# Pool's layer norm adds a negated mean instead of subtracting the mean, on one Trainium2 core

## The chip, the cores and the metric

The kernel runs on one core of one Trainium2 chip. The metric is the device time of one execution in microseconds (us). The engines are called PE (matmul), PEld (its weight loads), DVE (vector), ACT (scalar), Pool (GpSimd) and SP (which here only issues DMAs). Several chips were used. Kernels are compared with runs of the kernel before on the same chip, in the same rounds; where two runs of different chips are set side by side, the text says so. Faster, same, slower is taken at 2%, so a clear difference below that counts as "same".

## The reference, cut to what matters

The input x is 2048 tokens by 448 features. It is layer-normalised once (xn) and then goes through a linear-attention branch and an MLP-mixer branch that has a second layer norm.

```python
def _layernorm(x, axis=-1, eps=1e-5):
    m = jnp.mean(x, axis=axis, keepdims=True)
    v = jnp.var(x, axis=axis, keepdims=True)
    return (x - m) / jnp.sqrt(v + eps)
...
x = A_x
xn = _layernorm(x, axis=-1)
return x + _A_ref(xn, ...) + _B_ref(xn, ...)     # _B_ref: x1 = xn + hs; gelu(_layernorm(x1) @ w3) @ w4
```

## The kernel before

The tokens are 16 tiles of 128. One layer norm of a tile is: statistics on DVE (`bn_stats`, `bn_aggr`), variance plus epsilon on DVE, the power -1/2 on Pool, and the apply (x - mean) * rstd, which is one instruction on DVE or on Pool.

```python
def ln_stats(stt, mvt, src, i):
    R.ew(dve, "bn_stats", stt[:, i, 0:6], src[:, i, 0:D])
    R.ew(dve, "bn_aggr", mvt[:, i, 0:2], stt[:, i, 0:6])

def ln_scale(mvt, rst, a, n):
    R.ew(dve, "tensor_scalar", mvt[:, a:a + n, 2], mvt[:, a:a + n, 1], LN_EPS, 1.0, op0=ALU.add, op1=ALU.mult)
    R.ew(pool, "tensor_tensor", rst[:, a:a + n, 0], mvt[:, a:a + n, 2], mhalf[:, 0:n], op=ALU.pow)

def ln_apply(eng, dst, src, mvt, rst, i):
    R.ew(eng, "tensor_scalar", dst, src, mvt[:, i, 0:1], rst[:, i, 0:1], op0=ALU.subtract, op1=ALU.mult)
```

In the first norm DVE applies tiles 0 to 3. From tile 4 on, tiles go in pairs, and Pool applies the even tile of each pair (6 applies) and DVE the odd one. In the second norm Pool does all 16 applies; their results are called g_tok. SP transposes g_tok by DMA into gT, which feeds the w3 matmuls.

```python
for i in range(4, NT, 2):
    ln1_stats(i, 2)
    ln1_apply(i, 1, [pool])
    if i > 4:
        ln1_apply(i - 1, 1, [dve])
ln1_apply(NT - 1, 1, [dve])
...
def g_apply(i):
    ln_apply(pool, halves(g_tok[:, i % 4, :]), lap(xn[:, i, :]), mv2, rs2, i)
def g_T(i):
    R.dma_t(gT[:, (i // 4) % 2, :, j:j + 128], g_tok[:, i % 4, :])
```

Most tiles of xn are transposed by PE, but tiles 12 to 15 go by DMA, at the end of the first norm. The normalising of phik and of the attention output (o_tok, a part of the tile xnT) are also Pool's work.

The softmax here doesn't subtract the row's maximum and nothing guards it: scores larger than these inputs give would overflow.

Of the kernel before, what the change touches and what calls it, by code (L numbers as in the profile page):

```python
# [5 lines left out]
ACT = mybir.ActivationFunctionType  # L6
ALU = mybir.AluOpType
# [4 lines left out]
LN_EPS = 1e-5  # L12
# [5 lines left out]
class Recorder:  # L18
# [183 lines left out]
    def dma_t(self, out, in_, eng="SP"):  # L202
        self.op(eng, lambda e: e.dma_start_transpose(out, in_), [out], [in_], dma=True)

    def dma(self, out, in_, eng="SP"):
        self.op(eng, lambda e: e.dma_start(out, in_), [out], [in_], dma=True)


def bass_parallel_sum__linear_kernel_hedgehog__mixer_s_mlp__prompt_kernel(
# [6 lines left out]
    NT, NG, KC, NC, NM, FC, HP = 16, 4, 4, 4, 4, 14, 32  # L216
# [6 lines left out]
    with es:  # L223
        R = Recorder(nc, es)
# [13 lines left out]
        def new(name, cols, dt=BF16):  # L238
            return view(region(name, cols * DTB[dt]), cols, dt)
# [9 lines left out]
        xtok = new("xtok", NT * D).rearrange("p (t d) -> p t d", t=NT)  # L249
        xn = new("xn", NT * 512).rearrange("p (t d) -> p t d", t=NT)  # L250
# [13 lines left out]
        wv = new("wv", KC * D).rearrange("p (c d) -> p c d", c=KC)  # L264
# [17 lines left out]
        mv = new("mv", NT * 8, F32).rearrange("p (t c) -> p t c", t=NT)  # L282
        rs = new("rs", NT * 8, F32).rearrange("p (t c) -> p t c", t=NT)
        st2 = new("st2", NT * 8, F32).rearrange("p (t c) -> p t c", t=NT)
        mv2 = new("mv2", NT * 8, F32).rearrange("p (t c) -> p t c", t=NT)
        rs2 = new("rs2", NT * 8, F32).rearrange("p (t c) -> p t c", t=NT)
        ksum = new("ksum", 4 * 32, F32).rearrange("p (b c) -> p b c", b=4)
        rks = new("rks", 4 * 32, F32).rearrange("p (b c) -> p b c", b=4)
        mhalf = new("mhalf", 8, F32)
# [33 lines left out]
        dve, pool = "DVE", "POOL"  # L323
# [6 lines left out]
            R.dma(dst[:, 0:3, :], src[0:384, :].rearrange("(c p) d -> p c d", p=128))  # L330
            R.dma(dst[0:64, 3, :], src[384:448, :])

        def load_lap(dst, src, eng="SP"):
            R.dma(dst[:, 0:2, :], src[0:256, :].rearrange("(c p) d -> p c d", p=128), eng)
            R.dma(dst[:, 2:4, :], src[192:448, :].rearrange("(c p) d -> p c d", p=128), eng)

        load_x(0, 1)
# [13 lines left out]
        def load_rest():  # L351
# [7 lines left out]
        kq = kvq[0:CR, :, :].rearrange("p b (h e) -> p b h e", e=HP)  # L359

        R.op("ACT", lambda e: e.preload_act_table_set("gelu_apprx_tanh_and_others"), [], [])
        load_lap(wv, A_wqkv[:, 896:1344], "ACT")
        R.ew(pool, "memset", ident[:, :], 0.0)
        R.op(pool, lambda e: e.affine_select(ident[:, :], ident[:, :], pattern=[[-1, 128]],
                                             compare_op=ALU.not_equal, fill=1.0, base=0, channel_multiplier=1),
             [ident], [ident])
        R.ew(pool, "memset", mhalf[:, :], -0.5)
        R.ew(pool, "memset", hT[:, :, 0:2], 0.0)
        R.ew(pool, "memset", hT[:, :, S + 2:S + 4], 0.0)
        R.ew(pool, "memset", vp[:, 0:8 * H, DH:HP], 0.0)  # L370
        R.ew(pool, "memset", vp[:, 0:8 * H, DH:DH + 1], 1.0)
        def masks():
            R.ew(pool, "memset", rsel[0:DH, :], 0.0)
            R.op(pool, lambda e: e.affine_select(rv, rv, pattern=[[0, 4], [-1, DH]], compare_op=ALU.not_equal,
                                                 fill=1.0, base=0, channel_multiplier=1), [rsel[0:DH, :]], [rsel[0:DH, :]])
            R.ew(pool, "memset", maskb[0:CR, :], 1.0)
            R.op(pool, lambda e: e.affine_select(mb, mb, pattern=[[-DH, 4], [0, DH]], compare_op=ALU.is_ge,
                                                 fill=0.0, base=0, channel_multiplier=1), [maskb[0:CR, :]], [maskb[0:CR, :]])
            R.op(pool, lambda e: e.affine_select(mb, mb, pattern=[[DH, 4], [0, DH]], compare_op=ALU.is_ge,
                                                 fill=0.0, base=DH - 1, channel_multiplier=-1),  # L380
                 [maskb[0:CR, :]], [maskb[0:CR, :]])
# [12 lines left out]
        def lap(a):  # L394
            return bass.AP(a.tensor, a.offset, [list(a.ap[0]), [192, 2], [1, 256]])

        def halves(a):
            return a.rearrange("p (b e) -> p b e", b=2)

        def ln_stats(stt, mvt, src, i):  # L400
            R.ew(dve, "bn_stats", stt[:, i, 0:6], src[:, i, 0:D])
            R.ew(dve, "bn_aggr", mvt[:, i, 0:2], stt[:, i, 0:6])

        def ln_scale(mvt, rst, a, n):
            R.ew(dve, "tensor_scalar", mvt[:, a:a + n, 2], mvt[:, a:a + n, 1], LN_EPS, 1.0, op0=ALU.add, op1=ALU.mult)
            R.ew(pool, "tensor_tensor", rst[:, a:a + n, 0], mvt[:, a:a + n, 2], mhalf[:, 0:n], op=ALU.pow)

        def ln_apply(eng, dst, src, mvt, rst, i):
            R.ew(eng, "tensor_scalar", dst, src, mvt[:, i, 0:1], rst[:, i, 0:1], op0=ALU.subtract, op1=ALU.mult)

        def ln1_stats(a, n):
            for i in range(a, a + n):
                ln_stats(st, mv, xtok, i)
            ln_scale(mv, rs, a, n)

        def ln1_apply(a, n, engs):
            for i in range(a, a + n):
                ln_apply(engs[i % len(engs)], halves(xn[:, i, :]), lap(xtok[:, i, :]), mv, rs, i)


        def phi_blocks():
# [13 lines left out]
        def xn_T(i, b):  # L435
            b = banks[b]
            for kc in range(KC):
                R.tr(tview(b)[:, 128 * kc:128 * kc + 128], xn[:, i, 128 * kc:128 * kc + 128], ident[:, :])
            R.act(xnT[:, :, 128 * i:128 * i + 128], tview(b).rearrange("p (c d) -> p c d", c=KC), ACT.Copy)
# [39 lines left out]
        def kq_quad(i, bs):  # L479
            g, c = divmod(i, 4)  # L480

            def outs(k):
                return banks[bs[k]][:, 0:D] if k < 2 else banks[bs[k]][0:CR, :]

            def lhs(k, kc, lo, hi):
                if k < 2:
                    return xnT[lo:hi, kc, 128 * (i + k):128 * (i + k) + 128]
                return wpq[lo:hi, kc, CR * (c + k - 2):CR * (c + k - 1)]

            def rhs(k, kc, lo, hi):  # L490
                return wpk[lo:hi, kc, :] if k < 2 else xnT[lo:hi, kc, 512 * g:512 * g + 512]

            quad(outs, lhs, rhs)
            for s in range(2):
                R.act(phik[:, i:i + 2, s, :], two(bs[0])[:, :, 0:D], ACT.Exp, scale=1.0 - 2.0 * s)
            e = (eq_lo if g < 2 else eq_hi)[0:CR, c:c + 2, :, 512 * (g % 2):512 * (g % 2) + 512]
            for s in range(2):
                R.act(e[:, :, s, :], two(bs[2])[0:CR, :, :], ACT.Exp, scale=1.0 - 2.0 * s)
# [41 lines left out]
        def g_apply(i):  # L540
            ln_apply(pool, halves(g_tok[:, i % 4, :]), lap(xn[:, i, :]), mv2, rs2, i)
# [71 lines left out]
            R.dma(out2d[128 * i:128 * i + 128, :], outb[:, i % 4, :])  # L613


        for i in range(4):
            ln1_stats(i, 1)
            if i > 0:
                ln1_apply(i - 1, 1, [dve])
        ln1_apply(3, 1, [dve])  # L620
        masks()
        for i in range(4, NT, 2):
            ln1_stats(i, 2)
            ln1_apply(i, 1, [pool])
            if i > 4:
                ln1_apply(i - 1, 1, [dve])
        ln1_apply(NT - 1, 1, [dve])
        xn_T(0, 0)
        xn_T(1, 1)
        v_quad(0, (4, 5, 6, 7), ([(xn_T, 2, 2)], [(xn_T, 3, 3)]))  # L630
# [11 lines left out]
        def take(n):  # L642
            r = [2 * ((ring[0] + k + 2) % 3) for k in range(n // 2)]
            ring[0] += n // 2
            return [b + j for b in r for j in (0, 1)]
# [3 lines left out]
        for ps in range(8):  # L649
            kq_quad(2 * ps, take(4))  # L650
            if ps in kvs:
                kv_tile(kvs[ps][0])
            late = [(kv_tile, i) for i in kvs.get(ps, (0, 0) if ps else (0,))[1:]]
            if ps in w2s:
                b = take(2)
                for i in w2s[ps]:
                    w2_tile(i, b[i % 2], False)
                    for f in late[0:1]:
                        f[0](*f[1:])
                    late = late[1:]  # L660
                k_norm(2 * ps)
                for i in w2s[ps]:
                    ln_stats(st2, mv2, xn, i)
                    if i % 4 == 3:
                        ln_scale(mv2, rs2, i - 3, 4)
            else:
                v_quad(8 if ps == 1 else 12, take(4), (late,))
                k_norm(2 * ps)
                g_apply(ps - 1)
                g_apply(ps)  # L670
            if ps in (2, 4):
                g_T(ps - 2)
                g_T(ps - 1)
        N, W, O, G, St, Ff, Fo = num_tile, w2_tile, o_T, g_T, store, fin_full, fin_out
# [3 lines left out]
                g_apply(4 * g + j)  # L678

        def sc(g):  # L680
            ln_scale(mv2, rs2, 4 * g, 4)

        plan = [
            [(kv_tile, 13), (W, 14), (kv_tile, 14), (ga, 1)],
            [(kv_tile, 15), (kv_copy,), (W, 15), (sc, 3), (G, 4), (G, 5)],
            [(kv_blocks,), (G, 6), (G, 7), (ga, 2)],
            [(N, 0), (O, 0)],
            [(G, 8), (G, 9), (N, 1), (O, 1), (Ff, 0), (N, 2), (O, 2)],
            [(G, 10), (G, 11), (N, 3), (O, 3), (Ff, 1)],
            [(N, 4), (O, 4), (Ff, 2), (St, 0), (N, 5), (O, 5), (Ff, 3), (St, 1)],  # L690
            [(ga, 3), (N, 6), (O, 6), (Ff, 4), (St, 2), (St, 3)],
            [(G, 12), (G, 13), (G, 14), (G, 15), (N, 7), (O, 7), (Ff, 5)],
            [(N, 8), (O, 8), (Ff, 6), (St, 4), (N, 9), (O, 9), (Ff, 7), (St, 5)],
            [(N, 10), (O, 10), (Ff, 8), (St, 6)],
            [(N, 11), (O, 11), (St, 7), (Ff, 9), (N, 12), (O, 12)],
# [20 lines left out]
        for h in range(2):  # L716
            c = slice(224 * h, 224 * h + 224)
# [32 lines left out]
```

## Time and profile before

The time before was 205.26 us (median of three runs, 204.25 to 205.37). The profiled run took 203.74 us, with a span of 202.0 us.

| stage of the span (us) | PE idle (us) | what PE waits for |
|---|---|---|
| 0 to 6 | 5.8 | the first x tile and its norm |
| 6 to 33 | 4.1 | xn tiles, from Pool and DVE, then their DMA transposes |
| 33 to 57 | 0.6 | |
| 57 to 113 | 3.7 | DVE xn, gT, xnT |
| 113 to the end | 4.0 | mostly the tail after the last matmul (2.9) |

The idle times are the width of a stretch less PE's busy time in it. They are a little too large where matmul records are missing: this trace has 1103 of them, and what seems idle in front of a group can be a matmul without a record. The first line below is from part 1 of the page (busy us, share of the span, instructions).

```profile
PE 183.7 (91%) x1103; PEld 91.5 (45%) x1113; DVE 111.5 (55%) x273; ACT 81.5 (40%) x95; POOL 123.9 (61%) x129
```

The lines of PE's waits that matter (who was waited for; total us, times, longest):

```profile
PE bank L192 <- DVE xn L200: 6.4, 2, 5.8
PE bank L188 <- DMA xnT<-xn: 1.8, 1, 1.8
PE bank L188 <- DMA gT<-g_tok: 1.3, 1, 1.3
PE bank L188 <- DVE bd L200: 1.1, 1, 1.1
PE bank L188 <- DMA xnT<-xnT: 1.0, 1, 1.0
...
PE bank L188 <- DVE xn L200: 0.6, 1, 0.6
```

The Pool groups that matter (busy us, mean ns of one):

```profile
L200 POOL TENSOR_SCALAR g_tok<-xn,mv,rs 128x512 bf16<-128x512 bf16 x16 | 33.0, 2074 | 0.0
...
L200 POOL TENSOR_SCALAR xn<-xtok,mv,rs 128x512 bf16<-128x512 bf16 x6 | 13.1, 2189 | 0.6
```

Pool's loop in the first norm, from the timeline (start, duration):

```profile
14.57 2.21 POOL L200 TENSOR_SCALAR xn<-xtok,mv,rs 128x512 bf16<-128x512 bf16 x1
16.75 0.71 POOL L200 TENSOR_TENSOR rs<-mv,mhalf 128x2 f32<-128x2 f32 x1
17.56 2.21 POOL L200 TENSOR_SCALAR xn<-xtok,mv,rs 128x512 bf16<-128x512 bf16 x1
```

Two tiles take 3.0 us here because Pool has no gap. DVE needs about 2.1 us for its part of a pair, so Pool sets the pace, and the xn of the last tile is ready at 28.8 us.

### The profile page before, as it was taken

What the parts mean: (1) busy time and instruction counts of PE and PEld (TensorE: products, weight loads), DVE (VectorE), ACT (ScalarE), POOL (GpSimd) and SP (SyncE); (2) the same over time, 40 slices, a digit from 0 to 9 for tenths busy, and PEclk for the clock granted to TensorE, in tenths of its full rate; (3) what the DMA queues carried; (4) which work ended last, traced back from release to release, by engine and by line L of the source; (5) the groups of instructions that cost most, each with busy time, mean ns of one, the idle gap of its engine ahead of it and who ended that gap; (6) DMA issues with size and microseconds to landing.
All of it is one profiled execution on the core that took longest, in us unless ns stands there. A gap on an engine that the chain in (4) does not pass through costs nothing.

```text
span 202.0 us, 2864 instructions
## 1 busy us (share of the span) xinstructions
PE 183.7 (91%) x1103; PEld 91.5 (45%) x1113; DVE 111.5 (55%) x273; ACT 81.5 (40%) x95; POOL 123.9 (61%) x129
## 2 busy tenths in 40 slices
PE   0798976999999999899698999999999999999994
PEld 0454543443544555544243544544445445454451
DVE  3897510089987999995244446451464416756031
ACT  2347776967563667843333123031230302303000
POOL 5689993007597999889997440799507144266230
PEclk9999999999999999999999999999999999999999
DMA  6994037970011020002201641220532120321211
GB/s 195 365 165 86 5 65 205 381 229 0 2 24 31 0 52 0 0 3 51 53 0 26 81 82 24 52 49 0 121 80 52 49 49 1 76 49 49 71 49 45
DMA packets 32939, 14.74 MB, mean 73 GB/s; under 512 B 24670, under 2 KB 32414, under 8 KB 32926
## 3 DMA queue, kind: packets, MB, share of 16 engines
q1 hardware_dynamic: 32238, 14.04, 27.9%
q10 hardware_dynamic: 688, 0.52, 0.8%
q8 instruction: 9, 0.15, 0.3%
q14 instruction: 4, 0.03, 0.1%
HBM read 7.08 MB, written 1.84 MB: 44 GB/s over the span
## 4 chain that ended last, share of the span: by engine, by line
PE 55%; POOL 21%; DVE 15%; DMA 4%; ACT 2%; issue 1%; SPq 1%; DVEq 0%
PE bank L188 55%; POOL g_tok L200 8%; POOL xn L200 7%; DVE ksum L200 4%; DVE st L200 3%; POOL rs L200 3%; DVE xn L200 3%; POOL phik L200 3%; DVE mv L200 2%; DVE vaug L200 2%; DMA xtok<-in_A_x_dram 2%; DVE rks L200 1%; DMA xnT<-xn 1%; DMA xnT<-xnT 1%; ACT eq_lo L196 1%
## 5 line engine op out<-in xcount | busy, mean ns | idle before, releaser
L196 ACT ACTIVATE phik<-bank 128x1024 bf16<-128x1024 f32 (+1 forms) x44 | 40.9, 982 | 90.1 <-PE bank L188 90.1
L200 DVE TENSOR_TENSOR vaug<-bank,vaug 128x464 f32<-128x464 f32 (+3 forms) x65 | 32.7, 513 | 31.3 <-PE bank L188 29.7
L188 PE MATMUL bank<-gT,w 128*128 128x512 bf16 (+1 forms) x214 | 44.9, 380 | 3.1 <-DMA gT<-g_tok 1.3
L188 PE MATMUL bank<-w,phik 128*128 128x448 bf16 x224 | 45.1, 353 | 0.8 <-DVE vaug L200 0.8
L200 POOL TENSOR_TENSOR xnT<-vaug 128x196 bf16<-128x196 f32 (+1 forms) x32 | 18.1, 585 | 39.9 <-DVE vaug L200 39.9
L200 POOL TENSOR_TENSOR phik<-phik,rks 128x896 bf16<-128x896 bf16 x16 | 26.8, 1696 | 18.9 <-DVE rks L200 18.9
L200 POOL TENSOR_SCALAR g_tok<-xn,mv,rs 128x512 bf16<-128x512 bf16 x16 | 33.0, 2074 | 0.0
L188 PEld LDWEIGHTS bank<-w,phik 128*128 128x128 bf16 x224 | 21.0, 98 | 20.2 <-DVE vaug L200 1.7
L188 PEld LDWEIGHTS bank<-gT,w 128*128 128x128 bf16 (+1 forms) x224 | 17.6, 97 | 26.9 <-issue 7.7
L200 POOL TENSOR_TENSOR vaug<-xn,xtok 128x448 f32<-128x448 bf16 x16 | 16.4, 1030 | 5.1 <-DVE vaug L200 5.1
L200 DVE TENSOR_TENSOR xn<-bank,xn 128x256 bf16<-128x256 f32 (+1 forms) x32 | 10.5, 380 | 14.1 <-PE bank L188 14.0
L200 DVE RECIPROCAL vaug<-bank 128x16 f32<-128x16 f32 x16 | 4.1, 255 | 25.4 <-PE bank L188 25.4
L200 DVE TENSOR_REDUCE ksum<-phik 128x32 f32<-128x896 bf16 x16 | 16.8, 1052 | 0.0
L188 PE MATMUL bank<-xnT,w 128*112 128x512 bf16 (+1 forms) x64 | 15.1, 386 | 1.8 <-DMA xnT<-xn 1.8
L188 PE MATMUL bank<-wo,xnT 128*128 128x448 bf16 (+1 forms) x64 | 14.5, 352 | 1.0 <-DMA xnT<-xnT 1.0
L188 PE MATMUL bank<-xnT,wpq 128*112 128x512 bf16 (+1 forms) x64 | 14.9, 381 | 0.3 <-ACT eq_lo L196 0.3
L188 PE MATMUL bank<-wv,xnT 128*128 128x448 bf16 (+1 forms) x64 | 14.5, 388 | 0.0
L188 PE MATMUL bank<-w,hT 112*128 112x448 bf16 x64 | 14.3, 353 | 0.0
L200 POOL TENSOR_TENSOR rs<-mv,mhalf 128x2 f32<-128x2 f32 (+2 forms) x14 | 10.9, 779 | 5.1 <-DVE mv L200 5.0
L200 POOL TENSOR_SCALAR xn<-xtok,mv,rs 128x512 bf16<-128x512 bf16 x6 | 13.1, 2189 | 0.6
L188 PE MATMUL bank<-wpk,xnT 128*128 128x448 bf16 (+1 forms) x64 | 13.3, 355 | 0.0
L192 PE MATMUL bank<-ident,xn 128*128 128x128 bf16 x48 | 5.3, 250 | 7.0 <-DVE xn L200 6.4
(57 smaller groups left out, 179.6 us busy)
## 6 DMA issues: line engine op xcount, KB each, us to landing
w<-in_B_w_dram SPq DMA_DIRECT2D x2, 896.0 KB, 5.8
out_dram<-vaug SPq DMA_DIRECT2D x15, 112.0 KB, 1.9
w<-in_B_w_dram SPq DMA_DIRECT2D x1, 1568.0 KB, 10.7
xtok<-in_A_x_dram SPq DMA_DIRECT2D x3, 448.0 KB, 5.8
wv<-in_A_wqkv_dram ACTq DMA_DIRECT2D x2, 224.0 KB, 3.2
w<-in_B_w_dram SPq DMA_DIRECT2D x2, 224.0 KB, 5.1
wo<-in_A_wo_dram SPq DMA_DIRECT2D x2, 224.0 KB, 6.8
w<-in_B_w_dram SPq DMA_DIRECT2D x1, 392.0 KB, 7.8
```

The costliest lines, as they stand in the source:

```text
L188: self.op("PE", lambda e: e.matmul(out, lhsT, rhs, start=start, stop=stop, skip_group_check=True), [out], [lhsT, rhs])
L192: self.op("PE", lambda e: e.transpose(out, in_, ident), [out], [in_, ident])
L196: self.op("ACT", lambda e: e.activation(out, in_, func, **kw), [out], [in_] + aps)
L200: self.op(eng, lambda e: getattr(e, name)(out, *args, **kw), [out], aps)
```

## The change

The intent is to shorten Pool's applies. The mean is negated once on Pool (a small instruction), and the apply is add then multiply. In addition all epsilon-adds move from DVE to Pool, the load of wv waits for a Pool constant so that it stays out of the way of the first x tiles, and in three steps of the plan the gT transposes are queued behind the o transposes.

```diff
-        def ln_scale(mvt, rst, a, n):
-            R.ew(dve, "tensor_scalar", mvt[:, a:a + n, 2], mvt[:, a:a + n, 1], LN_EPS, 1.0, op0=ALU.add, op1=ALU.mult)
+        def ln_scale(mvt, rst, a, n, neg):
+            R.ew(pool, "tensor_scalar", mvt[:, a:a + n, 2], mvt[:, a:a + n, 1], LN_EPS, 1.0, op0=ALU.add, op1=ALU.mult)
             R.ew(pool, "tensor_tensor", rst[:, a:a + n, 0], mvt[:, a:a + n, 2], mhalf[:, 0:n], op=ALU.pow)
+            if neg:
+                R.ew(pool, "tensor_scalar", rst[:, a:a + neg, 1], mvt[:, a:a + neg, 0], -1.0, 0.0, op0=ALU.mult,
+                     op1=ALU.add)
         def ln_apply(eng, dst, src, mvt, rst, i):
-            R.ew(eng, "tensor_scalar", dst, src, mvt[:, i, 0:1], rst[:, i, 0:1], op0=ALU.subtract, op1=ALU.mult)
+            m, op = (mvt[:, i, 0:1], ALU.subtract) if eng == dve else (rst[:, i, 1:2], ALU.add)
+            R.ew(eng, "tensor_scalar", dst, src, m, rst[:, i, 0:1], op0=op, op1=ALU.mult)
...
-        load_lap(wv, A_wqkv[:, 896:1344], "ACT")
...
         R.ew(pool, "memset", mhalf[:, :], -0.5)
+        load_lap(wv, A_wqkv[:, 896:1344], "ACT", mhalf)
...
-            [(G, 8), (G, 9), (N, 1), (O, 1), (Ff, 0), (N, 2), (O, 2)],
-            [(G, 10), (G, 11), (N, 3), (O, 3), (Ff, 1)],
+            [(N, 1), (O, 1), (Ff, 0), (G, 8), (G, 9), (N, 2), (O, 2)],
+            [(N, 3), (O, 3), (Ff, 1), (G, 10), (G, 11)],
... (G 12 to 15 likewise; the rest of the diff passes the new arguments through)
```

More of the change, by code (lines that the diff above doesn't have):

```diff
@@ L203, in dma_t, with dma @@
         self.op(eng, lambda e: e.dma_start_transpose(out, in_), [out], [in_], dma=True)
-    def dma(self, out, in_, eng="SP"):
-        self.op(eng, lambda e: e.dma_start(out, in_), [out], [in_], dma=True)
+    def dma(self, out, in_, eng="SP", behind=None):
+        self.op(eng, lambda e: e.dma_start(out, in_), [out], [in_] if behind is None else [in_, behind], dma=True)
 def bass_parallel_sum__linear_kernel_hedgehog__mixer_s_mlp__prompt_kernel(
@@ L331, in load_rows, with load_lap @@
             R.dma(dst[0:64, 3, :], src[384:448, :])
-        def load_lap(dst, src, eng="SP"):
-            R.dma(dst[:, 0:2, :], src[0:256, :].rearrange("(c p) d -> p c d", p=128), eng)
+        def load_lap(dst, src, eng="SP", behind=None):
+            R.dma(dst[:, 0:2, :], src[0:256, :].rearrange("(c p) d -> p c d", p=128), eng, behind)
             R.dma(dst[:, 2:4, :], src[192:448, :].rearrange("(c p) d -> p c d", p=128), eng)
@@ L402, in ln_stats, with ln1_stats, ln1_apply @@
             R.ew(dve, "bn_aggr", mvt[:, i, 0:2], stt[:, i, 0:6])
-        def ln_scale(mvt, rst, a, n):
-            R.ew(dve, "tensor_scalar", mvt[:, a:a + n, 2], mvt[:, a:a + n, 1], LN_EPS, 1.0, op0=ALU.add, op1=ALU.mult)
+        def ln_scale(mvt, rst, a, n, neg):
+            R.ew(pool, "tensor_scalar", mvt[:, a:a + n, 2], mvt[:, a:a + n, 1], LN_EPS, 1.0, op0=ALU.add, op1=ALU.mult)
             R.ew(pool, "tensor_tensor", rst[:, a:a + n, 0], mvt[:, a:a + n, 2], mhalf[:, 0:n], op=ALU.pow)
+            if neg:
+                R.ew(pool, "tensor_scalar", rst[:, a:a + neg, 1], mvt[:, a:a + neg, 0], -1.0, 0.0, op0=ALU.mult,
+                     op1=ALU.add)
         def ln_apply(eng, dst, src, mvt, rst, i):
-            R.ew(eng, "tensor_scalar", dst, src, mvt[:, i, 0:1], rst[:, i, 0:1], op0=ALU.subtract, op1=ALU.mult)
-        def ln1_stats(a, n):
+            m, op = (mvt[:, i, 0:1], ALU.subtract) if eng == dve else (rst[:, i, 1:2], ALU.add)
+            R.ew(eng, "tensor_scalar", dst, src, m, rst[:, i, 0:1], op0=op, op1=ALU.mult)
+        def ln1_stats(a, n, neg):
             for i in range(a, a + n):
                 ln_stats(st, mv, xtok, i)
-            ln_scale(mv, rs, a, n)
-        def ln1_apply(a, n, engs):
-            for i in range(a, a + n):
-                ln_apply(engs[i % len(engs)], halves(xn[:, i, :]), lap(xtok[:, i, :]), mv, rs, i)
+            ln_scale(mv, rs, a, n, neg)
+        def ln1_apply(eng, i):
+            ln_apply(eng, halves(xn[:, i, :]), lap(xtok[:, i, :]), mv, rs, i)
         def phi_blocks():
@@ L613, in store @@
             R.dma(out2d[128 * i:128 * i + 128, :], outb[:, i % 4, :])
-        for i in range(4):
-            ln1_stats(i, 1)
-            if i > 0:
-                ln1_apply(i - 1, 1, [dve])
-        ln1_apply(3, 1, [dve])
+        ln1_stats(0, 1, 0)
+        ln1_stats(1, 1, 0)
+        ln1_apply(dve, 0)
+        for i in (2, 3):
+            ln1_stats(i, 1, 0)
+            ln1_apply(dve, i - 1)
+        ln1_apply(dve, 3)
         masks()
         for i in range(4, NT, 2):
-            ln1_stats(i, 2)
-            ln1_apply(i, 1, [pool])
+            ln1_stats(i, 2, 1)
+            ln1_apply(pool, i)
             if i > 4:
-                ln1_apply(i - 1, 1, [dve])
-        ln1_apply(NT - 1, 1, [dve])
+                ln1_apply(dve, i - 1)
+        ln1_apply(dve, NT - 1)
         xn_T(0, 0)
@@ L664, in bass_parallel_sum__linear_kernel_hedgehog__mixer_s_mlp__prompt_kernel @@
                     if i % 4 == 3:
-                        ln_scale(mv2, rs2, i - 3, 4)
+                        ln_scale(mv2, rs2, i - 3, 4, 4)
             else:
@@ L680, in sc @@
         def sc(g):
-            ln_scale(mv2, rs2, 4 * g, 4)
+            ln_scale(mv2, rs2, 4 * g, 4, 4)
         plan = [
@@ L687, in bass_parallel_sum__linear_kernel_hedgehog__mixer_s_mlp__prompt_kernel @@
             [(N, 0), (O, 0)],
-            [(G, 8), (G, 9), (N, 1), (O, 1), (Ff, 0), (N, 2), (O, 2)],
-            [(G, 10), (G, 11), (N, 3), (O, 3), (Ff, 1)],
+            [(N, 1), (O, 1), (Ff, 0), (G, 8), (G, 9), (N, 2), (O, 2)],
+            [(N, 3), (O, 3), (Ff, 1), (G, 10), (G, 11)],
             [(N, 4), (O, 4), (Ff, 2), (St, 0), (N, 5), (O, 5), (Ff, 3), (St, 1)],
             [(ga, 3), (N, 6), (O, 6), (Ff, 4), (St, 2), (St, 3)],
-            [(G, 12), (G, 13), (G, 14), (G, 15), (N, 7), (O, 7), (Ff, 5)],
+            [(N, 7), (O, 7), (Ff, 5), (G, 12), (G, 13), (G, 14), (G, 15)],
             [(N, 8), (O, 8), (Ff, 6), (St, 4), (N, 9), (O, 9), (Ff, 7), (St, 5)],
```

## The prediction

> **What bounds the kernel now.** The page gives PE 183.7 us busy of a 202.0 us span at full granted clock, so only 18.3 us of PE idle time exist. By windows view and PE timeline: 5.8 us before the first transpose; 0.7 us in 6-13; 3.5 us in 13-33; 0.6 us in 44-57; 3.7 us in 57-113; 1.2 us in 113-185. PE is the limit from 33 to 57 and after 113. In the two stages where it waits, the chain of waits runs through Pool:
> - 10.9-28.7: Pool repeats "power 0.71 us, layer-norm apply 2.21 us" every 3.0 us for two tiles; DVE needs about 2.1 us per pair. It ends in the last transposing DMAs and a 1.8 us PE stall at 32.8.
> - 86.6-109: Pool does two phik multiplies, four g_tok applies (8.2 us), a power, four more applies, the first o_tok. PE stalls 1.34 us for gT and 1.01 us for xnT (waits view).
>
> **What the change does, with costs.**
> - Pool's 22 applies (6 x 2.19, 16 x 2.07 us = 46 us, groups view) go from subtract-multiply to add-multiply.[...] 2.07 us for 512 columns looks slow: a two-input Pool multiply of 896 columns takes 1.70 us.[...] Estimate: 1.0 us (0.6 to 1.4) if faster, 75% likely.
> - Ten small Pool negations and fourteen epsilon-adds come in, estimated 0.2 to 0.4 us each (tiny Pool copies: 0.20 us). Pool per pair: 3.0 to about 2.3 us. If add is not faster: 3.6 us.
> - DVE loses 14 epsilon-adds: 0.15-0.17 us alone, but 0.38-0.66 us when Pool is in an apply, ending with Pool's instruction.[...] First tiles: DVE's cycle 1.27 to about 1.12 us.
> - wv issues about 0.7 us later and leaves bandwidth to the first x tiles: the second lands at 4.35 us, I expect 0.2-0.5 us earlier. wv is first used at 7.3 us.
> - The gT transposing DMAs queue behind the o transposes in three steps; small help.
>
> **On the critical path (add fast).** Start 0.3; 6-33: about 3.0 of 4.1 us idle; 57-113: about 2.3 of 3.7 us; elsewhere 0, because PE is saturated. Sum 5.3 us. 205.3 - 5.3 = 200.0. If add is no faster, Pool's lengthened loop costs 3-4 us in the first stage and 1-2 us before 109: about 209. Weighted point: 200.5 us, range 198.0 to 206.0. Chances: faster 0.63, same 0.28, slower 0.09.
>
> **What would show it.** Groups view: apply on Pool near 1.0 us; Pool total 124 to about 105 us. Timeline: xn of the last tile done near 24-25 us instead of 28.8; PE wait for xnT<-xn gone or under 0.5 us; waits for gT<-g_tok and xnT<-xnT nearly gone; DVE epsilon-adds absent; PE busy still near 184 us. First PE at 5.4 us.
>
> **What would make it wrong.** Add as slow as subtract; small Pool operations costing 0.6 us like the power; DVE or ACT (15.6 of 20 us busy in 13-33) taking over as limit there; a late wv; new waits from the moved gT.

Three passages of this text, and one each of the expectations of a_eps, p_forms and a_warm, are cut where marked: they rested on things that no trace or run of this case shows. The text came to 5.3 us, from 0.3, 3.0 and 2.3 us (which add to 5.6, see below), and so to 205.3 - 5.3 = 200.0 us, then to 200.5 us weighted. The 1.0 us for an apply was the estimate; the number beside it, 1.70 us for 896 columns of the multiply, comes to 0.97 us for 512 (an estimate by the columns alone), and the 75% is judgement. Of the slow epsilon-adds on DVE, that of 0.66 us (at 83.33 us) lies beside Pool's phik multiplies and not beside an apply.

## The result, and the profile after

The kernel after took 197.05 us (median of four runs, 196.66 to 197.5), and before took 204.97 us in the median of all its four runs on that chip. The ratio is 0.9618 (95% interval 0.9579 to 0.9657): faster. A ratio here is the mean time of one kernel's runs over that of the other's of the same rounds, so it is not quite the ratio of the quoted medians.

Part 1 of the page after:

```profile
PE 183.0 (94%) x1113; PEld 91.8 (47%) x1113; DVE 108.1 (55%) x259; ACT 81.1 (41%) x95; POOL 99.4 (51%) x153
```

PE's waits after, the four longest:

```profile
PE bank L192 <- DVE xn L200: 6.6, 2, 5.1
PE bank L188 <- DVE vaug L200: 0.8, 5, 0.2
PE bank L188 <- ACT phik L196: 0.7, 2, 0.4
PE bank L188 <- DMA xnT<-xn: 0.7, 1, 0.7
```

The same Pool groups, and the two kinds of small instruction that are new:

```profile
L200 POOL TENSOR_SCALAR g_tok<-xn,rs 128x512 bf16<-128x512 bf16 x16 | 12.1, 772 | 0.0
...
L200 POOL TENSOR_SCALAR xn<-xtok,rs 128x512 bf16<-128x512 bf16 x6 | 4.8, 798 | 0.6
...
L200 POOL TENSOR_SCALAR mv<-mv 128x2 f32<-128x2 f32 x6 | 1.2, 194 | 0.9 <-DVE mv L200 0.5
L200 POOL TENSOR_SCALAR rs<-mv 128x1 f32<-128x1 f32 x6 | 1.1, 192 | 0.5
```

Pool's loop in the first norm after, one period:

```profile
14.69 0.77 POOL L200 TENSOR_SCALAR xn<-xtok,rs 128x512 bf16<-128x512 bf16 x1
15.54 0.19 POOL L200 TENSOR_SCALAR mv<-mv 128x2 f32<-128x2 f32 x1
15.82 0.70 POOL L200 TENSOR_TENSOR rs<-mv,mhalf 128x2 f32<-128x2 f32 x1
16.60 0.19 POOL L200 TENSOR_SCALAR rs<-mv 128x1 f32<-128x1 f32 x1
16.90 0.77 POOL L200 TENSOR_SCALAR xn<-xtok,rs 128x512 bf16<-128x512 bf16 x1
```

PE does the same work, 183 us. The apply went from 2.07 to 0.77 us, and a pair from 3.0 to 2.2 us. Pool's busy time fell by 24.5 us, but the span fell by only 6.5 us, because PE, busy for 183.0 us of the 195.5, limits the rest. Where those 6.5 us arose is read from the start times of the same PE instructions in the two timelines:

| PE instruction | before (us) | after (us) | gained so far (us) |
|---|---|---|---|
| first transpose of xn | 5.79 | 5.14 | 0.65 |
| first w1 quad | 13.00 | 12.71 | 0.29 |
| last w1 quad (after the DMA transposes) | 32.76 | 29.43 | 3.33 |
| first w3 quad | 84.87 (a record missing) | 80.78 | 4.09 (too large) |
| phik group after the first w3 quad | 87.88 | 84.00 | 3.88 |
| fifth w3 quad | 103.69 | 98.32 | 5.37 |
| first wo matmul | 111.20 | 104.66 | 6.54 |
| last group of wo matmuls | 198.23 | 191.70 | 6.53 |

The row of the first w3 quad misleads. Its line before has 15 matmuls where the line after has 16, so the first record is missing, and the start shown is some 0.2 us late:

```profile
84.87 3.08 PE L188 MATMUL bank<-gT,w 128*128 128x512 bf16 x15 [0.61 <-DVE xn L200]
...
80.78 3.29 PE L188 MATMUL bank<-gT,w 128*128 128x512 bf16 x16
```

So 3.3 us come by the end of the first norm, 0.55 us (3.88 - 3.33) at the first w3 quad (PE's wait for DVE xn is gone), 1.5 us (5.37 - 3.88) at the gT wait and 1.2 us at the first o_tok. After that there is nothing.

At the end of the first norm PE waits in both kernels for the last of the four transposing DMAs of tiles 12 to 15. Pool's last apply ends 4.5 us earlier (28.76 to 24.29 us), and SP issues the last of those DMAs 4.0 us earlier (30.02 to 26.00 us): in the kernel after all four follow each other every 1.3 us, without waiting for Pool. PE starts 3.3 us earlier. So not all of Pool's gain arrives.

Two things needed an explanation. The traces differ by 6.5 us but the first medians by 7.9 (204.97 against 197.05). And the earlier first transpose (0.65 us) is nearly all given back by the first w1 quad.

### The profile page after: what moved, and what is told of

Its sections match the earlier page's. It is cut to its first block, busy times and chain, and to the rows that moved or that the text cites. A ratio compares the mean times of both kernels' runs of the same rounds, so it can differ in the third digit from the quotient of the medians.

```text
span 195.5 us, 2884 instructions
## 1 busy us (share of the span) xinstructions
PE 183.0 (94%) x1113; PEld 91.8 (47%) x1113; DVE 108.1 (55%) x259; ACT 81.1 (41%) x95; POOL 99.4 (51%) x153
## 4 chain that ended last, share of the span: by engine, by line
PE 77%; POOL 7%; DVE 5%; DMA 4%; ACT 3%; issue 2%; SPq 1%; DVEq 0%
PE bank L188 77%; POOL rs L200 3%; POOL xn L200 2%; DMA xtok<-in_A_x_dram 2%; ACT phik L196 2%; DVE vaug L200 2%; DMA xnT<-xn 2%; DVE st L200 1%; ACT eq_lo L196 1%; POOL phik L200 1%; POOL mv L200 1%; DVE xn L200 1%; SPq L203 1%; DVE ksum L200 1%; SPq L206 0%
## 5 line engine op out<-in xcount | busy, mean ns | idle before, releaser
L188 PE MATMUL bank<-gT,w 128*128 128x512 bf16 (+1 forms) x224 | 46.1, 380 | 0.7 <-ACT phik L196 0.7
L188 PE MATMUL bank<-xnT,w 128*112 128x512 bf16 (+1 forms) x64 | 15.1, 386 | 0.7 <-DMA xnT<-xn 0.7
L200 POOL TENSOR_SCALAR g_tok<-xn,rs 128x512 bf16<-128x512 bf16 x16 | 12.1, 772 | 0.0
L200 DVE BATCH_NORM_STATS2 st<-xtok 128x6 f32<-128x448 bf16 x16 | 9.7, 609 | 3.7 <-DMA xtok<-in_A_x_dram 3.7
## 6 DMA issues: line engine op xcount, KB each, us to landing
w<-in_B_w_dram SPq DMA_DIRECT2D x1, 1568.0 KB, 10.9
```

The lines of the kernel that those rows point to most:

```text
L188: self.op("PE", lambda e: e.matmul(out, lhsT, rhs, start=start, stop=stop, skip_group_check=True), [out], [lhsT, rhs])
L200: self.op(eng, lambda e: getattr(e, name)(out, *args, **kw), [out], aps)
```

## The experiments

### 1. Which part is the gain: subtract put back, or add alone

Theory: the add form is the gain. Rival: the moves (epsilon off DVE, wv, the order of the transposes) are. Before took 203.59 us (203.50 to 203.85).

a_sub is the kernel after with:

```diff
-            m, op = (mvt[:, i, 0:1], ALU.subtract) if eng == dve else (rst[:, i, 1:2], ALU.add)
+            m, op = (mvt[:, i, 0:1], ALU.subtract)
-            if neg:
+            if False:
```

> The kernel after, with Pool's applies back to subtract-multiply and the negations gone; scales on Pool, wv behind the constant and the new order stay. Theory (the add form is the gain): Pool applies back at 2.07-2.2 us, Pool pair period in the first stage about 3.3 us (one more small Pool instruction than before), the xnT<-xn, gT and xnT<-xnT waits of PE back, time 204 to 207 us, 0.99 to 1.01 of before. Rival (the moves off DVE, of wv and of the gT transposes are the gain): 199 us or less.

b_add is the kernel before with the new apply and the negations only (`neg` is 1 for pairs, 4 for the second norm):

```diff
+            neg = 4 if n == 4 else 1 if n == 2 else 0
+            if neg: ... negation on Pool, as in the change
-            R.ew(eng, "tensor_scalar", dst, src, mvt[:, i, 0:1], rst[:, i, 0:1], op0=ALU.subtract, op1=ALU.mult)
+            m, op = (mvt[:, i, 0:1], ALU.subtract) if eng == dve else (rst[:, i, 1:2], ALU.add)
+            R.ew(eng, "tensor_scalar", dst, src, m, rst[:, i, 0:1], op0=op, op1=ALU.mult)
```

> The kernel before, with only the add form and its ten negations. Theory: applies 0.77 us, time 197 to 199.5 us, so at least 70% of the gain of 7.9 us. Rival: 203 us or more.

Measured: a_sub 206.61 us, ratio 1.0145 (interval 1.011 to 1.018), which is slower than before, though by less than 2%. b_add took 198.49 us, ratio 0.9743 (0.9714 to 0.9771), a gain of 5.1 us. The rival falls: without the add form all of the gain is gone, and alone it gives 5.1 us. (I had put 70% of 7.9, 5.5 us, as its floor; on this chip before was itself 1.4 us quicker, see experiment 5.)

a_sub also shows the price of the moves. Pool's loop with subtract and with the epsilon-add on Pool takes 3.39 us a pair instead of 3.0:

```profile
18.41 2.21 POOL L200 TENSOR_SCALAR xn<-xtok,mv,rs 128x512 bf16<-128x512 bf16 x1
20.70 0.19 POOL L200 TENSOR_SCALAR mv<-mv 128x2 f32<-128x2 f32 x1
20.97 0.72 POOL L200 TENSOR_TENSOR rs<-mv,mhalf 128x2 f32<-128x2 f32 x1
21.80 2.21 POOL L200 TENSOR_SCALAR xn<-xtok,mv,rs 128x512 bf16<-128x512 bf16 x1
```

### 2. The first norm and the second apart

a_ln1add and a_ln2add are the kernel after with add in one norm only:

```diff
# a_ln1add
-            m, op = (mvt[:, i, 0:1], ALU.subtract) if eng == dve else (rst[:, i, 1:2], ALU.add)
+            m, op = (mvt[:, i, 0:1], ALU.subtract) if eng == dve or mvt is mv2 else (rst[:, i, 1:2], ALU.add)
-            if neg:
+            if neg and mvt is mv:
# a_ln2add: mv and mv2 exchanged
```

> The kernel after, with add in the first layer norm's 6 applies and subtract in the second's 16. Theory: the first stage keeps its 3.3 us of gain at 33 us, the stage 57-113 loses its 3.2 us: about 200 to 201 us. Rival (the stages are not additive; once the first is early, the second no longer binds, or the second alone absorbs all): under 198.5 or over 203 us.

> The kernel after, with add in the second layer norm's 16 applies and subtract in the first's 6. Theory: the first stage is back at before or 0.5-1.5 us later, the second keeps 3.2 us: about 201 to 203 us, slower than the run with add in the first norm only. Rival (the stages are not additive): under 198.5 or over 204 us.

Measured: a_ln1add 200.2 us (ratio 0.9826), as expected; its PE waits beyond 40 us are 1.4 us for xnT<-xnT and 1.3 us for gT<-g_tok, just those that the second norm's add removes. a_ln2add took 204.3 us (ratio 1.0031), which is above the 201 to 203 us of the theory and, by 0.3 us, in the range of the rival. From a_sub, add in the first norm is worth 6.4 us and in the second 2.3 us in the medians. Those medians mix clocks, as the next paragraph shows: at like clocks it is some 5.8 us in the first norm (a_sub's two runs at clock 1.0, 205.89 and 206.03 us) and some 3.0 us in the second (its two at 0.992, 207.19 and 207.36 us).

The first norm is worth more here than the 3.3 us of the before-and-after comparison for two reasons. Its loop in a_sub is longer than before's by the epsilon-add. And a second effect shows in the clock: in the profiled run of a_sub PE was granted a clock of 0.50 for some 3.4 us after its wait for the last transposing DMA. The stretch from 33 to 44 us has a granted clock of 0.84 in the profiles of both a_sub and a_ln2add. The mean clock of all four runs of a_ln2add (0.991 to 0.992) and of two of the four of a_sub (0.992) suggests such a spell in each of them. The two slower runs of a_sub had spans of 205.5 us at clock 0.992, the other two 204.0 and 204.3 us at 1.0; so such a spell cost about 1.3 us. The windows view of a_sub (width, then busy us of PE, PEld, DVE, ACT and Pool, then granted PE clock, DMA share and GB/s) places it:

```profile
33.00:35.00 2.00, 0.23 (x1) 0.18 (x2) 0.00 (x0) 1.83 (x3) 0.96 (x8) 1.00 0.57 92
35.00:36.00 1.00, 1.00 (x8) 0.74 (x7) 0.00 (x0) 0.00 (x0) 0.00 (x0) 0.69 0.66 233
36.00:38.00 2.00, 2.00 (x10) 1.08 (x9) 0.00 (x0) 0.79 (x2) 0.00 (x0) 0.50 1.03 405
38.00:39.00 1.00, 1.00 (x8) 0.51 (x7) 0.00 (x0) 0.30 (x1) 0.00 (x0) 0.60 1.02 416
```

From the 0.69 and the 0.60 in this view the spell lies at about 35.4 to 38.8 us (an estimate), so it lasted some 3.4 us. PE's timeline agrees: in it four bd matmuls took 0.58 us, against 0.36 to 0.37 us on either side of it, and three of the w1 quad 1.45 to 1.48 us, against 0.81. The gap in front of the spell was 1.8 us of PE idle time. The gap alone does not decide it, since the kernel before has the same 1.8 us gap and no later run of it shows a spell (clock 0.998 or higher). a_sub has in addition a 1.9 us gap 5 us earlier, where before has 1.1 us. What brings a spell on was not tested.

### 3. The three moves, each put back

Before took 203.68 us (203.37 to 204.35). a_wv0 is the kernel after with `load_lap(wv, ..., "ACT")` at the start again; a_plan has the old order of the three plan steps; a_eps is:

```diff
-            R.ew(pool, "tensor_scalar", mvt[:, a:a + n, 2], mvt[:, a:a + n, 1], LN_EPS, 1.0, op0=ALU.add, op1=ALU.mult)
+            R.ew(dve, "tensor_scalar", mvt[:, a:a + n, 2], mvt[:, a:a + n, 1], LN_EPS, 1.0, op0=ALU.add, op1=ALU.mult)
```

> The kernel after with wv issued at the start as in before. Theory: within 0.4 us of after, because the first transpose starts 0.65 us earlier with the delay but tiles 2 and 3 then land later (5.94 us) and PE waits 1.41 us for them. Rival (the prediction's): the delay is worth 0.3 us or more, so this run is that much slower.

> The kernel after with the old order of the gT transposes. Theory: same within 0.3 us, since with Pool fast no PE wait for xnT<-xnT or gT is left to shorten. Rival: the order is worth 0.5 to 1.0 us, and the 1.0 us wait for xnT<-xnT comes back.

> The kernel after with all 14 epsilon-adds back on DVE. Theory[...]: DVE's four-column epsilon-adds take 0.5 to 1.3 us again while Pool multiplies phik, DVE falls behind, and PE's 1.6 us wait for DVE xn before the first w3 quad is back as in the run with the add form alone; the first stage ends about 0.3 us earlier; net 0.8 to 1.5 us slower than after. Rival (placement is neutral): within 0.4 us of after.

| run | median us | ratio to before, 95% interval |
|---|---|---|
| after_again (the kernel after) | 197.46 | 0.9693, 0.9671 to 0.9714 |
| a_wv0 | 196.69 | 0.9658, 0.9632 to 0.9683 |
| a_plan | 196.86 | 0.9662, 0.9641 to 0.9683 |
| a_eps | 198.91 | 0.9759, 0.9734 to 0.9785 |

wv: undoing the delay did not cost anything; the kernel was 0.8 us quicker in the median, with intervals that overlap a little. (My theories had a_wv0 within 0.4 us of after and a_plan within 0.3; a_plan was 0.6 us quicker, again with overlapping intervals. No trace explains these 0.6 to 0.8 us.) The prediction's 0.3 us of gain is not there. A likely reason shows on DVE in the kernel after: tile 1 came early, but tile 2 later than before (its statistics began at 5.64 us before, without a wait). In the other profiled runs with the same loads tile 2 began between 5.58 and 5.99 us.

```profile
3.62 0.59 DVE L200 BATCH_NORM_STATS2 st<-xtok 128x6 f32<-128x448 bf16 x1
...
5.96 0.63 DVE L200 BATCH_NORM_STATS2 st<-xtok 128x6 f32<-128x448 bf16 x1 [0.88 <-DMA xtok<-in_A_x_dram]
```

PE waited 1.41 us for tile 2 then, against 0.66 us before, and its second group of transposes began 0.12 us later than before (7.17 against 7.05 us). The 0.29 us of gain at the first w1 quad came back in the ten wv matmuls in front of it: these took 2.12 us after (from 10.66 us) and 2.53 us before (from 10.54 us), and the clock record turns to full at 10.9 us after and at 12.0 us before (see experiment 5). Nothing shows that the change caused that: in two repeats of the kernel after the ten took 2.54 and 2.39 us, and in b_add, where they start at 10.54 us as in before, 2.12 us.

Plan: no wait for gT or xnT<-xnT came back with the old order, and PE's waits beyond 40 us are the same list in a_plan as in after_again. The new order bought nothing that a run shows.

Epsilon: putting it back on DVE costs 1.4 us, and a_eps shows the wait of PE that comes back (first line). b_add, which also has epsilon on DVE, shows how. The line of its PE waits that is new (0.2 us of it is again a matmul without a record), then its longest epsilon-add on DVE's timeline, then Pool's timeline beside it:

```profile
PE bank L188 <- DVE xn L200: 1.4, 1, 1.4
...
PE bank L188 <- DVE xn L200: 1.6, 1, 1.6
```

```profile
68.66 1.26 DVE L200 TENSOR_SCALAR mv<-mv 128x4 f32<-128x4 f32 x1
69.83 1.27 DVE L200 TENSOR_TENSOR xn<-bank,xn 128x256 bf16<-128x256 f32 x4
```

```profile
66.53 3.36 POOL L200 TENSOR_TENSOR phik<-phik,rks 128x896 bf16<-128x896 bf16 x2
70.00 1.01 POOL L200 TENSOR_TENSOR rs<-mv,mhalf 128x4 f32<-128x4 f32 x1
```

An instruction on four columns took 1.26 us on DVE and ended at 69.92 us, 0.03 us after Pool's phik multiply (66.53 + 3.36 = 69.89 us). Another took 0.17 us in the kernel before, where Pool was idle:

```profile
49.65 0.17 DVE L200 TENSOR_SCALAR mv<-mv 128x4 f32<-128x4 f32 x1
```

The kernel before has more that ended with an instruction of Pool: one of 0.66 us at 83.33 us ended at 83.99 us, Pool's phik multiplies (from 77.25 us) at 83.97, and one of 0.38 us on two columns at 16.43 us ended at 16.81 us, Pool's apply at 16.78. Not every DVE instruction took longer beside Pool: in the kernel before, DVE's own apply at 12.38 us took its usual 0.40 us in the middle of an apply on Pool (11.69 to 13.77 us). What lengthens some of them was not tested. A second epsilon-add of b_add took 0.66 us at 80.59 us. Against 0.17 us each the two lost 1.6 us together. DVE has no gap between 64.4 and 84 us of its timeline, so this delay reached PE as the wait at the first w3 quad. On Pool the same epsilon-add takes 0.20 us.

### 4. The cost of the forms by themselves, and the epsilon-add of the first norm

p_forms is the kernel after with twelve `tensor_scalar` instructions on dead tiles at the end of Pool's stream:

```python
s, a, t = ALU.subtract, ALU.add, ALU.mult
for k, (o0, o1, s0, s1, w) in enumerate(
        [(s, t, mean, rstd, 512), (a, t, neg, rstd, 512), (s, t, 0.5, 2.0, 512), (t, a, rstd, neg, 512),
         (a, t, 0.5, 2.0, 512), (t, s, rstd, mean, 512), (s, s, mean, mean, 512), (a, a, neg, neg, 512),
         (a, s, neg, mean, 512), (t, t, rstd, rstd, 512), (s, t, mean, rstd, 256), (a, t, neg, rstd, 256)]):
    R.ew(pool, "tensor_scalar", g_tok[:, k % 4, 0:w], src[:, 0:w], s0, s1, op0=o0, op1=o1)
```

> The kernel after, with twelve Pool tensor-scalar instructions on dead tiles at its end, 512 columns bf16 to bf16: in order subtract-mult, add-mult (both per-partition), subtract-mult immediate, mult-add, add-mult immediate, mult-subtract, subtract-subtract, add-add, add-subtract, mult-mult, then subtract-mult and add-mult on 256 columns. Theory[...]: those with a subtract 1.9-2.1 us, those without 0.75-0.8 us, whatever the operands; at 256 columns about 1.1 and 0.45 us. Rival A (only add-mult is fast): mult-add, add-add, mult-mult slow too. Rival B (operand kind, not operation): immediates fast even with subtract.

Pool's timeline, in that order:

```profile
188.62 2.08 POOL L200 TENSOR_SCALAR g_tok<-xn,mv,rs 128x512 bf16<-128x512 bf16 x1
190.69 0.77 POOL L200 TENSOR_SCALAR g_tok<-xn,rs 128x512 bf16<-128x512 bf16 x1
191.43 1.92 POOL L200 TENSOR_SCALAR g_tok<-xn 128x512 bf16<-128x512 bf16 x1
193.34 0.77 POOL L200 TENSOR_SCALAR g_tok<-xn,rs 128x512 bf16<-128x512 bf16 x1
194.08 0.62 POOL L200 TENSOR_SCALAR g_tok<-xn 128x512 bf16<-128x512 bf16 x1
194.67 2.08 POOL L200 TENSOR_SCALAR g_tok<-xn,rs,mv 128x512 bf16<-128x512 bf16 x1
196.74 2.08 POOL L200 TENSOR_SCALAR g_tok<-xn,mv 128x512 bf16<-128x512 bf16 x1
198.80 2.10 POOL L200 TENSOR_SCALAR g_tok<-xn,rs 128x512 bf16<-128x512 bf16 x1
200.88 2.08 POOL L200 TENSOR_SCALAR g_tok<-xn,rs,mv 128x512 bf16<-128x512 bf16 x1
202.93 0.77 POOL L200 TENSOR_SCALAR g_tok<-xn,rs 128x512 bf16<-128x512 bf16 x1
203.69 1.23 POOL L200 TENSOR_SCALAR g_tok<-xn,mv,rs 128x256 bf16<-128x256 bf16 x1
204.90 0.55 POOL L200 TENSOR_SCALAR g_tok<-xn,rs 128x256 bf16<-128x256 bf16 x1
```

The fast pairs are add-mult, mult-add and mult-mult (0.77 us at 512 columns, 0.62 for add-mult with immediates). Every pair with a subtract is slow, with per-partition operands (2.08 us) or immediates (1.92 us). But add-add is slow too (eighth line, 2.10 us), which my theory had as fast. So "no subtract" is not the rule. Rival A and rival B fall as well. From 256 to 512 columns the fast form grows by 0.22 us, so 0.86 ns a column, and the slow one by 0.85 us, so 3.3 ns a column. These differences are from single instructions. The starts of the lines lie as far apart as the durations say (2.07 us after the first, 0.74 us after the second), so the two classes do not hang on how the profiler ends an instruction. What inside Pool makes the two classes is not tested.

c_eps1 is the kernel after with the epsilon-add on DVE for the pairs of the first norm only (`R.ew(dve if n == 2 else pool, ...)`), and d_wv0_eps1 also issues wv at the start.

> The kernel after with the epsilon-adds of the six tile pairs of the first norm on DVE, those of the first four tiles and of the second norm on Pool. Theory: Pool's pair loop shortens from 2.2 to 2.05 us, so the last tile's xn is 0.7-0.9 us earlier, while the 1.4 us DVE stall does not return; 0.3 to 0.7 us faster than after, if nothing else binds at 29 us. Rival (the end of the first stage is bound elsewhere): within 0.2 us of after.

> The run before with wv issued at the start in addition. Theory: the two gains add, 0.8 to 1.3 us faster than after, the best of all so far. Rival (both gain time for the same last transposing DMA, and PE saturates): no better than either alone, some 0.7 us faster than after.

Measured, with before at 203.73 us: c_eps1 196.80 us (ratio 0.9662, 0.9649 to 0.9676) and d_wv0_eps1 196.71 us (0.9662, 0.9648 to 0.9676). Pool's pair loop became 2.03 us, against 2.2. The kernel after was not run in this call; against its 197.3 to 197.5 us on two other chips c_eps1 is 0.5 to 0.7 us quicker, with ratios (0.9693 and 0.9687) whose intervals just overlap, so this gain is likely and not clear. The two gains do not add: the first line of that theory falls. Against a_eps (0.9759, from another chip), c_eps1 differs in the epsilon-adds of the second norm and of the first four tiles only, and is about 1% better. So Pool is the better place for the epsilon-add of the second norm, where DVE has no gap (64.4 to 84 us of b_add); in the pairs of the first norm, where Pool sets the pace, DVE may be a little better.

### 5. What was still open: the size of the gain, PE's slow start, tile 2

c_dma is c_eps1 with x tiles 2 and 3 in a DMA each and wv behind a memset of vaug. c_dma2 is its mended form:

```diff
-        load_x(2, 2)
+        load_x(2, 1)
+        load_x(3, 1)
...
-        load_lap(wv, A_wqkv[:, 896:1344], "ACT", mhalf)
...
+        R.ew(pool, "memset", vp[:, 0:8 * H, DH:HP], 0.0)          # moved up
         R.ew(pool, "memset", hT[:, :, 0:2], 0.0)
+        load_lap(wv, A_wqkv[:, 896:1344], "ACT", hT[:, 0, 0:2])
```

> Epsilon as in the first run of this call; x tiles 2 and 3 in a DMA each and wv behind a later Pool memset (about 2.4 us). Theory (PE waits for tile 2 because tiles 2 and 3 share one DMA with wv beside it): tile 2's bn_stats starts before 5.2 us, the second PE wait shrinks below 0.8 us, 0.3 to 0.8 us faster than with epsilon alone moved. Rival (the bandwidth is taken by later x and w1 loads, or wv now comes late): no gain, or a wait for wv after 7.5 us.

> c_dma mended: wv behind the first memset of hT, moved to about 2.4 us, which nothing rewrites. Theory: tile 2's bn_stats starts before 5.2 us (5.96 in after), first transpose near 5.1 us, second PE wait under 0.8 us, 0 to 0.5 us faster than the same without the DMA edits (196.8 us). Rival: wv late, PE waits for it after 7.5 us, slower.

c_dma took 198.47 us, slower by 1.7 us than c_eps1, through an error of mine. Pool's next memset rewrites the part of vaug that the load was made to read, so Pool had to wait for wv:

```profile
5.51 0.65 POOL L200 MEMSET vaug<- 128x128 bf16 x1 [3.27 <-DMA wv<-in_A_wqkv_dram]
```

c_dma2 waits on a constant that nobody rewrites. It took 196.31 us (195.95 to 196.39), ratio 0.9637 (0.9624 to 0.9649). The kernel after (after_third) took 197.31 us (196.88 to 197.56). Tile 2's statistics began at 5.02 us instead of 5.96, and PE's second wait is 0.45 us instead of 1.4:

```profile
5.02 0.62 DVE L200 BATCH_NORM_STATS2 st<-xtok 128x6 f32<-128x448 bf16 x1
```

So tile 2 came 0.94 us earlier when it did not share its DMA with tile 3 and wv came a little later still; the run changes both and does not tell them apart. This version beats both kernels, by 1.0 us and 7.4 us in medians. The 1.0 us includes the moved epsilon-adds: against c_eps1, which has those alone (ratio 0.9662, on another chip), the intervals just touch, so what the two edits of the loads give by themselves is not clear.

after_again and after_third repeat the kernel after unchanged:

> The kernel after, unchanged, beside before. The two profiles differ by 6.5 us, the first medians by 7.9. Theory: before's first timed runs (204.25 to 205.37 us, against 203.74 when profiled) held spells of halved PE clock after the 1.8 us PE gap near 31 us, as two later runs showed (3.4 us at half clock, 1.3 us of span); where before runs at granted clock 1.0 the gain is 6.5 to 7.0 us (ratio 0.966 to 0.968), and a before run with clock 0.992 is some 1.3 us longer. Rival: the ratio is 0.962 again with before at clock 1.0.

> The kernel after, unchanged, on a further chip. Theory: the change itself is worth what the traces differ by, 6.5 us, with launch-to-launch spread of 0.5 us from the start: ratio 0.965 to 0.970. Rival (the first session is typical): 0.962 or below. A before run at clock 0.992 would show that half-clock spells can lengthen it by 1.3 us.

The ratios are 0.9693 (0.9671 to 0.9714) and 0.9687 (0.9675 to 0.97), and before took 203.68 and 203.66 us. So on two further chips the gain is 6.2 and 6.4 us in medians, close to the 6.5 us of the traces, not 7.9. The difference is in before: in the first session it ran at 204.25 to 205.37 us, in four later calls, each on another chip, at 203.37 to 204.35 us. I suspected half-clock spells as in a_sub. Later every before run was at clock 0.998 or higher, so none shows one, and the clock of the first session's timed runs is not on record. That suspicion stays open.

a_warm is the kernel after with 32 idle matmuls before the first transpose; w_warm_t is d_wv0_eps1 with those and with tiles 14 and 15 transposed by PE instead of DMA:

```diff
+        for _ in range(32):
+            R.mm(banks[7][:, 0:128], ident[:, :], ident[:, :], True, True)
         ln1_stats(0, 1, 0)
... w_warm_t also
-        for i in range(12, 16):
+        for i in range(12, 14):
             xn_Td(i)
-        w1_quad(2, (4, 5, 6, 7), [[(fold, 1, m, m % 2)] for m in range(NM)])
+        w1_quad(2, (4, 5, 6, 7), [[(fold, 1, m, m % 2)] + ([(xn_T, 12 + m, m)] if m > 1 else []) for m in range(NM)])
```

> The kernel after with 32 idle 128x128 matmuls on the identity before the first transpose (1.5 to 5 us), into a bank that is overwritten later. Theory: [...]the first stage's end hangs on the last transposing DMAs at 29 us, so at most 0.4 us faster than after. Rival (cold PE sets the first stage): 1 us or more faster.

> wv at the start, the first norm's pair epsilon on DVE, the 32 idle matmuls, and tiles 14 and 15 transposed by PE and ACT in place of DMA. Theory (the last transposing DMAs end the first stage): the 0.3 to 1.1 us of PE waiting at 29 us goes, less 0.8 us of PE work added; 0.3 to 1.0 us faster than a_warm, the best of all. Rival (PE is full there anyway): no faster.

The background is that PE is slow at first (the "cold PE" of the rival): four transposes take 0.63 us in the kernel before at 10.11 us, and 0.40 us at 19.83 us, and the starts of transposes that follow each other lie 0.107 us apart at 7.1 us and 0.056 us at 15.1 us. The clock record of the profile turns to full at 12.0 us in before and at 10.9 us in after. (It begins with that turn, so its views print 1.00 for the time before it; the mean clock of a run does not show the slow start.) a_warm took 196.46 us (ratio 0.9648, 0.9635 to 0.966), against 0.9687 for after. But its six runs lie at 196.16 to 196.53 us with one at 197.89, and that one is the profiled run, in which PE became quick no earlier: the transposes at 10.45 us still took 0.63 us, and the ten wv matmuls from 10.87 us took 2.93 us, against 2.08 to 2.54 us in the other profiled runs whose start was read. So five runs are quicker, but the one that I can look into shows no earlier turn; why they are quicker is open. The median is 0.9 us below after's, more than the 0.4 us of the theory and just under the 1 us of the rival, so neither is settled. In the profiled run the idle matmuls ran from 1.6 to 5.2 us. That they would bring the turn forward was not shown, and no trace of a quicker run was kept. w_warm_t took 196.58 us (0.9666, 0.9641 to 0.9691), no better than a_warm, so the theory that the last DMA transposes still end the first stage is not supported. One of its runs took 198.35 us at clock 0.991; a run of a_warm with the same mean clock took 196.53 us, no longer than its neighbours.

## Why the prediction was wrong, point by point

The direction was right, and so was the reason, a shorter apply on Pool: 63% was given to "faster". The time was below the range: 197.05 against 198.0 to 206.0. Two terms of "205.3 - 5.3" failed. The term for 57-113 was 2.3 us and measured 3.2, mainly because the path from DVE's lengthened epsilon-adds (0.66 us for 0.17) to PE was left out. And the start value, 205.3 us, was 1.6 us above what before takes on other chips; the cause of that stays open. From the weighted 200.5 us, take 0.5 us for the weighting, 0.3 us for a slip in the sum, 0.9 us for 57-113 and 1.6 us for the start value, and 197.2 us are left, against 197.05 measured.

- **"Estimate: 1.0 us (0.6 to 1.4) if faster, 75% likely."** Faster it is, shown by b_add and p_forms. The size is 0.77 us, so better than the estimate. The small instructions cost 0.19 to 0.24 us each in the mean of their groups and 0.28 to 0.30 us with their gap in the loop, at the low end of the estimate.
- **"Pool per pair: 3.0 to about 2.3 us", "xn of the last tile done near 24-25 us".** Right: 2.2 us, and Pool's last apply ended at 24.3 us.
- **"Start 0.3; 6-33: about 3.0."** Right in sum: 3.3 us at the last w1 quad. But the part named for the start was not wv's: a_wv0 shows that the delay of wv gave nothing. That 0.29 us stood at the first w1 quad, as "Start 0.3" said, is luck: it came in the ten wv matmuls in front (2.12 us for 2.53), with the earlier turn of the clock. At the last w1 quad PE waits for a DMA in both kernels, so all 3.3 us there are what the DMA came earlier.
- **"57-113: about 2.3 of 3.7 us."** This is the term that was mis-sized: 6.54 - 3.33 = 3.2 us. The gT and xnT waits (2.35 us in the waits view) went wholly and gave 2.66 us in start times, and the wait for DVE xn before the first w3 quad went too and gave 0.55 us. I had listed DVE's lengthened epsilon-adds (0.38 to 0.66 us) but not followed them to PE. With the first stage earlier and epsilon left on DVE, that wait would have grown to 1.4 us (a_eps; 1.6 in b_add's view, with a record missing). a_eps prices the move at 1.4 us, and I gave it nothing on PE's path in this stage.
- **"Sum 5.3 us."** The three terms add to 5.6. This is a slip of arithmetic, 0.3 us.
- **"Weighted point: 200.5 us."** The possibility that add is no faster pulled the point up by 0.5 us, and it set the upper end of the range. The range below allowed 7.3 us of gain from 205.26.
- **The base.** The 205.26 us that I subtracted from was about 1.6 us above the 203.6 to 203.7 us that before took on four later chips, and above its own profiled run of 203.74 us. The 1.5 us between the profiled and the timed runs could be read before predicting, and I did not use it. Repeated, the gain is 6.2 to 6.4 us, against 5.6 from my terms. The excess of the first session's base is measured but its cause is open.
- **"The gT transposes queue behind the o transposes; small help."** Not shown: a_plan is no slower than after.

## What to carry to other kernels

On Pool, look at what an elementwise instruction costs per column before moving work away from it: the same layer-norm apply took 2.08 us as subtract-multiply and 0.77 us as add-multiply, and a 0.19 us negation pays for it. Put a small instruction on the engine that is not pacing that stage, and look at what runs beside it: a four-column DVE instruction took 1.26 us instead of 0.17 here and ended 0.03 us after a pair of Pool's multiplies (1.7 us each). Count the matmuls of a group before you trust the idle time in front of it. Before subtracting an expected gain from a time, compare the timed runs with the profiled one, and ask how much a different chip would give.
